# Head of a fused attention and MLP kernel: the first weight piece moved to ScalarE's queue, the first tiles reordered, two copies split, one constant's place in GpSimd's order changed

## The chip, the cores and the metric

The kernel runs on one core of a Trainium2 chip. A time is the device time of one execution in microseconds (us). The kernel before took 146.25 us, the median of three runs (146.13 to 146.31).

The core has five engines with a queue of instructions each: TensorE (PE: matmuls, and PEld for its weight loads), VectorE (DVE), ScalarE (ACT), GpSimd (POOL) and SyncE (SP, which here only issues DMAs). They meet through semaphores alone. Each engine takes its own instructions strictly in the order in which they were emitted, so an instruction that waits holds up everything behind it on its engine.

## The reference

One input x of 2048 tokens by 448 channels (bf16) is normalised, and two branches are computed from the result and added to x:

```
xn  = layernorm(x)
A   : q, k, v = xn @ wqkv (16 heads of 28); pq = q @ w_phi, pk = k @ w_phi (one 28x28 per head)
      phi = [softmax(p), softmax(-p)];  kv = phi_k^T v;  z = sum(phi_k)
      o = (phi_q kv) / (phi_q z + 1e-6);  A = o @ wo
B   : B = silu(xn @ w1) @ w2            (448 -> 1792 -> 448)
out = x + A + B
```

## The kernel before

Tokens are handled in 16 tiles of 128. The first tiles go a way of their own, the head; the rest of the work follows a list of blocks written out by hand (`PLAN`).

**Layer norm of a tile** (`ln_tile`, lines 699 to 744). VectorE computes the statistics (`bnst`, L702, and `bnag`, L703). For tiles 0 to 3 ScalarE takes the square root (`ve`, L706) and VectorE its reciprocal (`rstd`, L708); from tile 4 on GpSimd computes both `ve` (L711) and `rstd` (L713). VectorE then writes the normalised tile (`xn`, L717). Tiles 0 to 3 are turned over by TensorE, four transposes each (`tr`), which land in PSUM and are copied to `xnT` by ScalarE (`ev0a`, `ev0`, `ev1`, `ev2`) or, for tile 3, by VectorE (`ev3`). From tile 4 on, pairs of tiles are turned over by DMA transposes that SyncE issues (`xnT_dma5`, `xnT_dma7` and so on).

**The head on TensorE.** 38 matmuls of 128 columns on a tile of ones come first (`warm`, L586); nothing reads them. Then come the transposes, and, token tile by token tile, the first three blocks of `xn @ w1` (blocks 0, 1 and 2, two output tiles of 128 channels each). The order is one string (L1039): `00a` is block 0, token tile 0, contraction steps k = 0 and 1; `00b` is its last step, which takes k = 2 for one output tile and k = 3 for the other; `20` is block 2, tile 0, all steps. Blocks 0 and 1 read the first piece of w1 (columns 0 to 511), in two DMAs: `w1_0` (k = 0 and 1) and `w1_0r` (k = 2 and 3), 256 KB each. Block 2 reads the second piece, `w1_512` (k = 0 to 2, 384 KB) and `w1_512r` (k = 3, 128 KB).

**DMA issues.** SyncE issues, in this order, x0, x1 (112 KB each), x2 (tiles 2 and 3, 224 KB), w1_0, w1_0r, w1_512r, x4 (tiles 4 to 7, 448 KB), the rest of w1, the value weights, x8 and x12, and the transposes. ScalarE issues w1_512 behind its first activation table load and the small activation `warm_act`. GpSimd issues the four small loads of w_phi.

**The fold.** q and k are never formed: w_phi is folded into wqkv on the chip. GpSimd builds block-diagonal copies of w_phi (`bdphi`, L632, and `bd0`, L636), once the four loads of w_phi have landed. TensorE multiplies them with transposed pieces of wqkv (`fold_k`, words f0 and f1 in `PLAN`, L666), ScalarE copies out one reference column, and VectorE subtracts it (`fold_sub`, L695) into `Wqk`. Both f0 and f1 write PSUM banks 6 and 7, so f1 waits until f0's subtractions have read them.

**Order.** A small list scheduler (L228) puts the instructions in order by modelled times; its `chain` calls and the order of `PLAN` on TensorE are constraints on it. TensorE's order is fully written out. On VectorE, ScalarE and GpSimd it is written out for the first four tiles (L1025, L1026) and chosen by the scheduler's model behind them. GpSimd's order before has `bdphi` ahead of tile 4's `ve` and `bd0` ahead of its `rstd`. In `PLAN`, `aFn@b` and `bFn` are the two halves of block n of `xn @ w1`, seven blocks to each 512 tokens: F8 reads tiles 4 to 7, F25 reads tiles 12 to 15.

Of the kernel before, what the change touches and what calls it, by code (L numbers as in the profile page):

```python
# [358 lines left out]
SIGNAL = {("act", "pe"): 60.0, ("act", "dve"): 40.0, ("dve", "pe"): 100.0, ("dve", "sp"): 30.0, ("dve", "dve"): 34.0,  # L359
          ("pool", "pe"): 100.0}  # L360
PLAN = """r0 aF3@4 r2 r1 bF3 aF6@0 aF4@6 bF6 bF4 aF5@4 av2@2 av0@0 bv2 bF5 av4@6 bv0 bv4 aF10@2 aF9@0 bF10 f0@6 bF9 aF12@4 aF7@2
aF11@0 f1@6 bF11 bF7 bF12 aF25@0 ak2@6 bF25 bk2 av8@4 av12@2 bv8 ak0@0 bv12 bk0 av10@6 aF22@4 bv10 aF17@2 bF22 av14@6
aF14@0 bF17 bv14 aF18@4 bF14 aF27@6 ak4@2 bF27 bF18 bk4 av6@6 ak6@0 ak8@4 bv6 bk8 bk6 ak12@2 aF8@6 bk12 bF8 aY0@45
aF21@0 aY0 aF23@2 bF21 bF23 ak14@6 bY0 g0@1 bk14 bY0 aF13@0 aF19@2 bF13 aF20@4 bF19 aF24@6 bF20 bF24 ak10@0 g1@3 bk10 K0
K6 K4 aq4@2 K12 aq8@4 bq4 K8 K2 s4 aq0@0 bq8 aq6@2 K14 bq0 bq6 bY1@45 K10 M aY1 aq2@2 aF26@0 s6 bq2 bY1 bF26 aG3@23 aY1
aU2@67 s8 aF15@0 bU2 s0 bF15 aF16@4 bG3 bF16 aU4@01 aq12@6 bU4 bq12 aU3@45 bG3 bU3 s2 aG3 aq10@0 aq14@6 bq10 s10 aW2@45
# [5 lines left out]
def bass_parallel_sum__linear_kernel_hedgehog__dense_activation_silu__prompt_kernel(  # L372
# [36 lines left out]
    with es:  # L409
# [143 lines left out]
        def load(dst, src, name, eng="sp", lat=1700.0):  # L553
            n = 2
            for _, cnt in list(dst.ap):
                n *= cnt
            P.dma(lambda e: e.dma_start(out=dst, in_=src), n / 280.0, writes=[dst], name=name, eng=eng, lat=lat)  # L557
# [24 lines left out]
        memset(Wp0[:], 0.0, 28, "wp_zero")  # L582

        P.cur_prio = 9
        for i in range(38):
            o = P.op("pe", 107.0, lambda e: e.matmul(banks[3][:, 0:128], ones_bf[:], ones_bf[:], start=True, stop=True),  # L586
                 reads=[ones_bf[:]], writes=[banks[3][:, 0:128]], name="warm", mode=128)
            o.words = 2
# [10 lines left out]
        def load_w1(c0, c1, eng="sp"):  # L599
            load_rows4(w1_sb[:, :, c0:c1], B_w1, c0, c1, f"w1_{c0}", eng)  # L600
# [1 line left out]
        load_x(0, 1)  # L602
        load_x(1, 2)
        load_x(2, 4)
        load(w1_sb[:, 0:2, 0:512], B_w1[0:256, 0:512].rearrange("(k p) f -> p k f", p=128), "w1_0")
        load(w1_sb[:, 2:4, 0:512], bass.AP(B_w1.tensor, B_w1.offset + 256 * FF, [[FF, 128], [64 * FF, 2], [1, 512]]), "w1_0r")
        load_w1(512, 1024, "act")
        load_x(4, 8)
        load_w1(1024, FF)
        load_rows4(wv_sb, A_wqkv, 2 * D, 3 * D, "wv")  # L610
# [88 lines left out]
        def ln_tile(t):  # L699
            xs = x_sb[:, t, :]  # L700
            sl = t % NXN
            P.op("dve", 590, lambda e: e.bn_stats(st6[:, t, :], xs), reads=[xs], writes=[st6[:, t, :]], name=f"bnst{t}", okeys_w=["ln"])  # L702
            P.op("dve", 170, lambda e: e.bn_aggr(mv[:, t, :], st6[:, t, :]), reads=[st6[:, t, :]], writes=[mv[:, t, :]], name=f"bnag{t}",  # L703
                 okeys_w=["ln"])
            if t < 4:
                P.op("act", 220, lambda e: e.activation(ve[:, t:t + 1], mv[:, t, 1:2], ACTF.Sqrt, bias=epst[:]),  # L706
                     reads=[mv[:, t, 1:2], epst[:]], writes=[ve[:, t:t + 1]], name=f"ve{t}", table="sqrt", okeys_r=["sq"])
                P.op("dve", 120, lambda e: e.reciprocal(rstd[:, t:t + 1], ve[:, t:t + 1]),  # L708
                     reads=[ve[:, t:t + 1]], writes=[rstd[:, t:t + 1]], name=f"rstd{t}")
            else:  # L710
                P.op("pool", 200, lambda e: e.tensor_scalar(ve[:, t:t + 1], mv[:, t, 1:2], EPS_LN, None, ALU.add),  # L711
                     reads=[mv[:, t, 1:2]], writes=[ve[:, t:t + 1]], name=f"ve{t}")
                P.op("pool", 570, lambda e: e.tensor_tensor(rstd[:, t:t + 1], ve[:, t:t + 1], neghalf[:], ALU.pow),  # L713
                     reads=[ve[:, t:t + 1], neghalf[:]], writes=[rstd[:, t:t + 1]], name=f"rstd{t}")

            def norm(dst, c0, c1, dur, tag=""):
                P.op("dve", dur, lambda e: e.tensor_scalar(dst, x_sb[:, t, c0:c1], mv[:, t, 0:1], rstd[:, t:t + 1], ALU.subtract, ALU.mult),  # L717
                     reads=[xs, mv[:, t, 0:1], rstd[:, t:t + 1]], writes=[dst], name=f"xn{t}{tag}")

            dstx = xnT[:, t, :, :]  # L720
            if t >= XN_DMA0:
                norm(xn_sb[:, sl, 0:KF], 0, KF, 370)
                norm(xn_sb[:, sl, KF:512], D - 128, D, 250)
                if t % 2:
                    dma_t(xnT[:, t - 1:t + 1, :, :].rearrange("p i k c -> p (i k) c"),
                          xn_sb[:, sl - 1:sl + 1, :].rearrange("p i c -> p (i c)"), 950.0, f"xnT_dma{t}", 1330.0, lat=850.0)
                return

            def turn_over(k0, k1, b, tag):
                tps = bank16[b][:, 128 * k0:128 * k1].rearrange("p (k c) -> p k c", k=k1 - k0)  # L730
                transposes([(tps[:, kt - k0, :], xn_sb[:, sl, KS[kt]:KS[kt] + 128]) for kt in range(k0, k1)], f"tr{tag}")
                if t < 3:
                    act(dstx[:, k0:k1, :], tps, ACTF.Identity, 128 * (k1 - k0), f"ev{tag}")
                else:
                    copy(dstx[:, k0:k1, :], tps, 128 * (k1 - k0), f"ev{tag}")

            if t == 0:
                norm(xn_sb[:, sl, 0:256], 0, 256, 290, "a")
                norm(xn_sb[:, sl, 256:D], 256, D, 275)
                turn_over(0, 2, 4, "0a")  # L740
                turn_over(2, 4, 5, "0")
            else:
                norm(xn_sb[:, sl, 0:D], 0, D, 390)
                turn_over(0, 4, (7, 4, 5)[t - 1], str(t))

        LOW, HIGH = slice(0, 64), slice(64, 128)

# [274 lines left out]
            ln_tile(t)  # L1022
        fold()
        act(warm_act[:], ones_bf[:, 0:4], ACTF.Silu, 4, "silu_table", table="silu", okeys_w=["sq"])
        chain("bnst0 bnag0 bnst1 bnag1 rstd0 xn0a xn0 rstd1 xn1 bnst2 bnag2 bnst3 bnag3 rstd2 xn2 rstd3 xn3 ev3".split())  # L1025
        chain("warm_act w1_512 ve0 ve1 ev0a ev0 ev1 ve2 ve3 ev2 silu_table".split())  # L1026
        byname = {o.name: o for o in P.ops}
        byname["w1_512"].deps.add(byname["warm_act"].id)
        byname["w1_512"].odeps -= byname["w1_512"].deps
        fold_loads()  # L1030

        chunk = [(fp, c) for c in range(NCH) for fp in range(FP)]
# [3 lines left out]

        head = [F(0, 0), F(1, 2), F(2, AUX)]
        seq = []
        for word in "tr0a tr0 tr1 00a 10a 01a 11a 00b 10b 01b 11b tr2 20 21 tr3 02 12 22 03 13 23".split():  # L1039
            if word[0] == "t":  # L1040
                seq.append(word)
                continue
            f, t = int(word[0]), int(word[1])
            n0 = len(P.ops)
            head[f][0](t * 128, t * 128 + 128, {"": (0, 1, 2), "a": (0, 1), "b": (2,)}[word[2:]])
            for n, o in enumerate(P.ops[n0:]):
                o.name = f"F{word}_{n}"
                seq.append(o.name)
# [4 lines left out]
        block_mask(mask2[:], 2 * DH, 2, KP)  # L1053
        memset(vaug[:, :, :, DH], 1.0, 2150, "vaug1")
        memset(KVm[:], 0.0, 464, "kvm0")
        chain(["vaug1", "kvm0", "wphi", "wphi1", "wphi2", "wphi3"])
        def k_block(t, b0):
            return proj_block(t, b0, True)

# [12 lines left out]
        ones_column(NEK, NT)  # L1072
        for o in P.ops[-2:]:
            o.deps.add(late)

        prev = [max(o.id for o in P.ops if o.eng == "pe")]

# [177 lines left out]
```

## Time and profile before

| | |
|---|---|
| median of three runs | 146.25 us |
| the profiled execution: time, span | 146.72 us, 145.5 us |
| busy: PE, DVE, ACT, POOL | 97%, 62%, 55%, 52% |
| granted TensorE clock over the span | 1.000 |
| first matmul of `warm`, first transpose, first product with w1 | 1.06, 5.07, 6.10 us |
| last matmul's end, last addition on VectorE | 143.5, 143.9 us |

The span runs from the first to the last instruction of the profiled execution; its time is 1.22 us longer, and the profiled execution is 0.47 us above the median. Times in the lines of the profile count from the start of the span. In a line of the timeline the first number is the start, the second how long it or the run of like instructions took (their number is behind the x), and the brackets give the engine's idle time just before it and what ended that. A busy TensorE doesn't mean a useful one: the matmuls of `warm` count too.

### The profile page before, as it was taken

To read this page: it belongs to the slowest core of one execution; us is meant where nothing else is said; L and a number is where in the kernel's file an instruction comes from. 1 tells how busy PE (TensorE), PEld (TensorE's weight loads), DVE (VectorE), ACT (ScalarE), POOL (GpSimd) and SP (SyncE) were. 2 spreads that over 40 slices of the span, in tenths; PEclk is the share of its full clock that TensorE was granted. 3 is DMA by queue.
4 is the path that set the end of the run, shared out by engine and by line. 5 is a ranking of instruction groups with operands and counts; after the bars stand their busy time and mean duration, and the time that the engine had idled before them with its cause. 6 is when DMAs were issued, how large, how long until landed. Compare 5 with 4: busy or idle time off the path is not lost.

```text
span 145.5 us, 4553 instructions
## 1 busy us (share of the span) xinstructions
PE 141.3 (97%) x1968; PEld 83.0 (57%) x1968; DVE 89.5 (62%) x195; ACT 79.5 (55%) x96; POOL 75.2 (52%) x95
## 2 busy tenths in 40 slices
PE   7989999899999999999999999999999999999994
PEld 7785444345444544477787655555555556555773
DVE  1957899610770059948139999927796374635533
ACT  4567856379997899979896949246530000000000
POOL 8807477720097007799944999992398600000000
DMA  4999969654990000000000059959989999743522
GB/s 103 346 342 264 266 142 138 133 106 68 337 293 7 0 2 5 0 0 5 0 5 5 0 89 179 137 109 181 76 163 171 206 196 176 117 76 72 165 95 63
DMA packets 44500, 17.59 MB, mean 121 GB/s; under 512 B 36912, under 2 KB 44096, under 8 KB 44480
## 3 DMA queue, kind: packets, MB, share of 16 engines
q1 hardware_dynamic: 41648, 15.09, 53.0%
q10 hardware_dynamic: 2704, 2.19, 5.4%
q8 instruction: 15, 0.25, 0.7%
q0 software_dynamic: 128, 0.03, 0.1%
q14 instruction: 5, 0.04, 0.1%
HBM read 6.57 MB, written 1.84 MB: 58 GB/s over the span
## 4 chain that ended last, share of the span: by engine, by line
PE 68%; DVE 18%; POOL 5%; DMA 4%; issue 3%; ACT 1%; DVEq 0%; POOLq 0%; ACTq 0%
PE psum L520 68%; DVE Rec L837 7%; DMA Wp<-in_A_w_phi_dram 4%; DVE RA L717 4%; DVE st L702 3%; DVE Rec L838 2%; POOL rstd L713 1%; POOL Wp L557 1%; DVE mv L703 1%; POOL vaug L550 1%; DVE Wqk L695 1%; ACT Ek_sb L543 1%; POOL ve L711 1%; POOL BD L632 0%; DVE Y_sb L949 0%
## 5 line engine op out<-in xcount | busy, mean ns | idle before, releaser
L520 PE MATMUL psum<-xnT,phT 64*128 64x512 bf16 (+1 forms) x428 | 46.9, 350 | 0.6 <-DMA phT<-in_B_w_dram 0.4
L520 PE MATMUL psum<-w_sb,hT 64*128 64x448 bf16 (+4 forms) x455 | 46.5, 341 | 0.0
L837 DVE TENSOR_REDUCE Rec<-Ek_sb 128x32 f32<-128x896 bf16 (+1 forms) x20 | 24.4, 1251 | 18.7 <-ACT Ek_sb L543 18.6
L543 ACT ACTIVATE hT<-psum 128x1024 bf16<-128x1024 f32 x28 | 27.7, 1024 | 11.3 <-PE psum L520 11.2
L520 PEld LDWEIGHTS psum<-w_sb,hT 64*128 64x128 bf16 (+1 forms) x455 | 23.6, 94 | 17.2 <-issue 0.2
L520 PEld LDWEIGHTS psum<-xnT,phT 64*128 64x128 bf16 (+1 forms) x428 | 22.4, 95 | 19.0 <-DMA phT<-in_B_w_dram 0.6
L874 POOL TENSOR_TENSOR RA<-Ek_sb,Rec 128x896 bf16<-128x896 bf16 x16 | 27.1, 1723 | 5.7 <-DVE Rec L838 4.9
L520 PE MATMUL psum<-Wqk,xnT 64*128 64x432 bf16 x224 | 24.4, 342 | 0.0
L543 ACT ACTIVATE Ek_sb<-psum 128x864 bf16<-128x864 f32 x24 | 20.3, 917 | 6.3 <-PE psum L520 4.2
L847 POOL TENSOR_TENSOR Ek_sb<-Ek_sb,Rec 128x896 bf16<-128x896 bf16 x8 | 13.4, 1698 | 17.8 <-DVE Rec L838 17.8
L520 PEld LDWEIGHTS psum<-Wqk,xnT 64*128 64x128 bf16 x224 | 11.1, 94 | 8.2
L543 ACT ACT_TABLE_LOAD x11 | 14.1, 1283 | 1.0 <-PEq L1240 0.8
L847 POOL TENSOR_TENSOR phT<-phT,Rec 128x896 bf16<-128x896 bf16 x8 | 13.4, 1700 | 1.5 <-issue 0.9
L520 PE MATMUL psum<-wv,xnT 64*128 64x448 bf16 x112 | 12.2, 349 | 0.0
L1001 DVE TENSOR_TENSOR x_sb<-psum,x_sb 128x448 bf16<-128x448 f32 (+2 forms) x13 | 7.2, 583 | 7.5 <-PE psum L520 7.4
L702 DVE BATCH_NORM_STATS2 st<-x_sb 128x6 f32<-128x448 bf16 x16 | 9.7, 604 | 3.1 <-DMA x_sb<-in_A_x_dram 3.1
L520 PE MATMUL psum<-wo_sb,vaug 64*128 64x448 bf16 (+2 forms) x102 | 11.3, 338 | 0.0
L717 DVE TENSOR_SCALAR RA<-x_sb,mv,rstd 128x384 bf16<-128x384 bf16 (+4 forms) x29 | 9.0, 349 | 2.3 <-POOL rstd L713 2.1
L980 DVE TENSOR_TENSOR vaug<-psum,rden 128x448 bf16<-128x448 f32 x16 | 9.2, 619 | 0.0
L837 DVE TENSOR_REDUCE Rec<-phT 128x64 f32<-128x1792 bf16 x4 | 8.0, 1990 | 1.8 <-ACT phT L543 1.8
L838 DVE RECIPROCAL Rec<-Rec 128x32 f32<-128x32 f32 (+1 forms) x24 | 8.8, 396 | 0.2
L520 PEld LDWEIGHTS psum<-wv,xnT 64*128 64x128 bf16 x112 | 5.4, 94 | 5.6 <-ACT vaug L543 0.5
(60 smaller groups left out, 108.9 us busy)
## 6 DMA issues: line engine op xcount, KB each, us to landing
out_dram<-x_sb ACTq DMA_DIRECT2D x15, 112.0 KB, 2.4
w_sb<-in_B_w_dram SPq DMA_DIRECT2D x1, 1568.0 KB, 7.9
x_sb<-in_A_x_dram SPq DMA_DIRECT2D x3, 448.0 KB, 6.5
wo_sb<-in_A_wo_dram SPq DMA_DIRECT2D x2, 336.0 KB, 7.5
phT<-in_B_w_dram SPq DMA_DIRECT2D x1, 576.0 KB, 7.8
phT<-in_B_w_dram SPq DMA_DIRECT2D x2, 256.0 KB, 4.4
phT<-in_B_w_dram ACTq DMA_DIRECT2D x1, 384.0 KB, 4.7
wv<-in_A_wqkv_dram SPq DMA_DIRECT2D x1, 336.0 KB, 7.8
```

What stands on the lines that cost most here:

```text
L520: r = e.matmul(dst, lhsT, rhs, start=st, stop=sp, skip_group_check=True)
L543: P.op("act", d_act(n), lambda e: e.activation(dst, src, func, scale=scale), reads=[src], writes=[dst], table=table, name=name, **keys)
L550: P.op(eng, d_pool(n, 0.5), lambda e: e.memset(dst, v), writes=[dst], name=name)
L557: P.dma(lambda e: e.dma_start(out=dst, in_=src), n / 280.0, writes=[dst], name=name, eng=eng, lat=lat)
L702: P.op("dve", 590, lambda e: e.bn_stats(st6[:, t, :], xs), reads=[xs], writes=[st6[:, t, :]], name=f"bnst{t}", okeys_w=["ln"])
L717: P.op("dve", dur, lambda e: e.tensor_scalar(dst, x_sb[:, t, c0:c1], mv[:, t, 0:1], rstd[:, t:t + 1], ALU.subtract, ALU.mult), reads=[xs, ...
L837: P.op("dve", 50 + 967 * n, lambda e: e.tensor_reduce(R2, E4, AXL.X, ALU.add), reads=[E4], writes=[R2], name="Ssum")
L838: P.op("dve", 135 + 210 * n, lambda e: e.reciprocal(R2, R2), reads=[R2], writes=[R2], name="Rrec")
L847: P.op("pool", 1700, lambda e: e.tensor_tensor(E3, E3, Rk[:, :, None].broadcast_to([128, 32, DH]), ALU.mult), reads=[E3, Rk], writes=[E3], ...
L874: P.op("pool", 1700, lambda e: e.tensor_tensor(dst, Eq, Rq.rearrange("p (c j) -> p c j", c=CC)[:, :, :, None].broadcast_to([128, CC, 4, DH ...
L980: P.op("dve", 620, lambda e: e.tensor_tensor(o3, U3[:, :, 0:DH], rden[:, uq, :, None].broadcast_to([128, H, DH]), ALU.mult), reads=[U3[:, ...
L1001: P.op("dve", d_dve(cs.stop - cs.start), lambda e: e.tensor_tensor(res[:, cs], ob, addend[:, cs], ALU.add), reads=[ob, addend[:, cs]], wri ...
```

## The change

- The number of `warm` matmuls goes from 38 to 36.
- `w1_0` is issued by ScalarE, as its first instruction and ahead of its table load, once GpSimd's `ident` is done. `w1_512`, which ScalarE issued behind `warm_act`, goes to SyncE, between w1_0r and w1_512r.
- The copies of tiles 1 and 2 out of PSUM are split into two (`ev1a` and `ev1`, `ev2a` and `ev2`): k = 0 and 1, then k = 2 and 3.
- The order of the head on TensorE becomes tile 0 whole, tile 1, tile 2; tile 2's first part stands ahead of tile 3's transposes. On VectorE tile 3's `bnag` goes behind tile 2's `rstd` and `xn`.
- On GpSimd, `bdphi` and `bd0` go behind tile 7's `rstd`, and tile 8's `ve` behind them.
- In `PLAN`, F8 and F25 change places.

```diff
-aF11@0 f1@6 bF11 bF7 bF12 aF25@0 ak2@6 bF25 bk2 av8@4 av12@2 bv8 ak0@0 bv12 bk0 av10@6 aF22@4 bv10 aF17@2 bF22 av14@6
-aF14@0 bF17 bv14 aF18@4 bF14 aF27@6 ak4@2 bF27 bF18 bk4 av6@6 ak6@0 ak8@4 bv6 bk8 bk6 ak12@2 aF8@6 bk12 bF8 aY0@45
+aF11@0 f1@6 bF11 bF7 bF12 aF8@0 ak2@6 bF8 bk2 av8@4 av12@2 bv8 ak0@0 bv12 bk0 av10@6 aF22@4 bv10 aF17@2 bF22 av14@6
+aF14@0 bF17 bv14 aF18@4 bF14 aF27@6 ak4@2 bF27 bF18 bk4 av6@6 ak6@0 ak8@4 bv6 bk8 bk6 ak12@2 aF25@6 bk12 bF25 aY0@45
...
-        for i in range(38):
+        for i in range(36):
...
-        load(w1_sb[:, 0:2, 0:512], B_w1[0:256, 0:512].rearrange("(k p) f -> p k f", p=128), "w1_0")
+        load(w1_sb[:, 0:2, 0:512], B_w1[0:256, 0:512].rearrange("(k p) f -> p k f", p=128), "w1_0", "act")
...
-        load_w1(512, 1024, "act")
+        load_w1(512, 1024)
...
-            def turn_over(k0, k1, b, tag):
+            def turn_over(k0, k1, b, tag, cut=None):
...
-                if t < 3:
-                    act(dstx[:, k0:k1, :], tps, ACTF.Identity, 128 * (k1 - k0), f"ev{tag}")
-                else:
-                    copy(dstx[:, k0:k1, :], tps, 128 * (k1 - k0), f"ev{tag}")
+                for a, b, part in ((k0, k1, ""),) if cut is None else ((k0, cut, "a"), (cut, k1, "")):
+                    if t < 3:
+                        act(dstx[:, a:b, :], tps[:, a - k0:b - k0, :], ACTF.Identity, 128 * (b - a), f"ev{tag}{part}")
+                    else:
+                        copy(dstx[:, a:b, :], tps[:, a - k0:b - k0, :], 128 * (b - a), f"ev{tag}{part}")
...
-                turn_over(0, 4, (7, 4, 5)[t - 1], str(t))
+                turn_over(0, 4, (7, 4, 5)[t - 1], str(t), 2 if t < 3 else None)
...
-        chain("bnst0 bnag0 bnst1 bnag1 rstd0 xn0a xn0 rstd1 xn1 bnst2 bnag2 bnst3 bnag3 rstd2 xn2 rstd3 xn3 ev3".split())
-        chain("warm_act w1_512 ve0 ve1 ev0a ev0 ev1 ve2 ve3 ev2 silu_table".split())
+        chain("bnst0 bnag0 bnst1 bnag1 rstd0 xn0a xn0 rstd1 xn1 bnst2 bnag2 bnst3 rstd2 xn2 bnag3 rstd3 xn3 ev3".split())
+        chain("w1_0 warm_act ve0 ve1 ev0a ev0 ev1a ve2 ev1 ve3 ev2a ev2 silu_table".split())
         byname = {o.name: o for o in P.ops}
-        byname["w1_512"].deps.add(byname["warm_act"].id)
-        byname["w1_512"].odeps -= byname["w1_512"].deps
+        byname["w1_0"].deps.add(byname["ident"].id)
+        byname["w1_0"].xfer, byname["w1_0"].lat = 0.0, 2800.0
...
-        for word in "tr0a tr0 tr1 00a 10a 01a 11a 00b 10b 01b 11b tr2 20 21 tr3 02 12 22 03 13 23".split():
+        for word in "tr0a tr0 tr1 00a 10a 00b 10b 01a 11a 01b 11b tr2 20 21 02a tr3 12a 22a 02b 12b 22b 03 13 23".split():
...
+        chain(["rstd7", "bdphi", "bd0", "ve8"])
```

The lines that set `xfer` and `lat` change only what the scheduler believes of that DMA. The `chain` of `vaug1` to `wphi3` moves in the file with the same names in it.

More of the change, by code (lines that the diff above doesn't have):

```diff
@@ L1055, in bass_parallel_sum__linear_kernel_hedgehog__dense_activation_silu__prompt_kernel @@
         memset(KVm[:], 0.0, 464, "kvm0")
-        chain(["vaug1", "kvm0", "wphi", "wphi1", "wphi2", "wphi3"])
         def k_block(t, b0):
@@ L1074, in bass_parallel_sum__linear_kernel_hedgehog__dense_activation_silu__prompt_kernel @@
             o.deps.add(late)
+        chain(["vaug1", "kvm0", "wphi", "wphi1", "wphi2", "wphi3"])
+        chain(["rstd7", "bdphi", "bd0", "ve8"])
         prev = [max(o.id for o in P.ops if o.eng == "pe")]
```

## The prediction, made before the result was known

> **What bounds the kernel now.** First the page: which engine is full.
>
> ```profile
> span 145.5 us, 4553 instructions
> PE 141.3 (97%) x1968; PEld 83.0 (57%) x1968; DVE 89.5 (62%) x195; ACT 79.5 (55%) x96; POOL 75.2 (52%) x95
> ```
>
> TensorE is busy almost throughout, so a gain must come from its idle time or from work taken off it. Taken off are two `warm` matmuls of 107 ns. Its waits name the idle time:
>
> ```profile
> PE psum L520 <- DMA phT<-in_B_w_dram: 0.4, 1, 0.4
> PE psum L520 <- DVE Wqk L695: 0.4, 1, 0.4
> ```
>
> Since matmul ends are modelled, I measure gaps from start to start, against a step of 0.056 us for 128 columns and 0.216 for 512. From 5.7 us to the end three gaps exceed 0.24 us by that measure: 0.25 at 6.79 and 0.56 at 7.82 in the head, and 0.54 at 27.88. The timeline shows them with their causes:
>
> ```profile
> 0.80 1.28 ACT L543 ACT_TABLE_LOAD   x1 [0.80 <-PEq L1240]
> ...
> 2.10 0.20 ACT L543 ACTIVATE warm_act<-ones_bf 128x4 f32<-128x4 bf16 x1
> 2.20 1.46 SPq L557 DMA_DIRECT2D phT<-in_B_w_dram  x3
> 2.33 0.43 ACTq L557 DMA_DIRECT2D phT<-in_B_w_dram  x1
> ...
> 3.83 0.29 ACT L706 ACTIVATE ve<-mv,epst 128x1 f32<-128x1 f32 x1 [1.53 <-DVE mv L703]
> ...
> 6.10 1.31 PE L520 MATMUL psum<-xnT,phT 128*128 128x128 bf16 x16
> ...
> 6.79 0.45 PEld L520 LDWEIGHTS psum<-xnT,phT 128*128 128x128 bf16 x8 [0.26 <-ACT xnT L543]
> ...
> 7.82 0.62 PE L520 MATMUL psum<-xnT,phT 128*128 128x128 bf16 x8 [0.40 <-DMA phT<-in_B_w_dram]
> ```
>
> At 6.10 the first product starts just behind w1_0, whose last part the trace lands at 5.97; at 6.79 TensorE waits for ScalarE's copy of tile 1; at 7.82 for w1_0r, landed at 7.77. The third gap comes from a chain that starts on GpSimd:
>
> ```profile
> 11.62 0.56 POOL L632 TENSOR_TENSOR BD<-Wp,mask_half 128x224 bf16<-128x224 bf16 x1 [4.80 <-DMA Wp<-in_A_w_phi_dram]
> ...
> 12.16 0.23 POOL L711 TENSOR_SCALAR ve<-mv 128x1 f32<-128x1 f32 x1
> ...
> 12.61 0.57 POOL L713 TENSOR_TENSOR rstd<-ve,neghalf 128x1 f32<-128x1 f32 x1
> ...
> 13.22 0.60 DVE L717 TENSOR_SCALAR RA<-x_sb,mv,rstd 128x384 bf16<-128x384 bf16 x2 [0.91 <-POOL rstd L713]
> ```
>
> ```profile
> 26.71 1.12 DVE L695 TENSOR_TENSOR Wqk<-psum,last_k 128x432 bf16<-128x432 f32 x2
> ```
>
> ```profile
> 27.88 0.20 PE L520 MATMUL psum<-BD,Y_sb 64*128 64x56 bf16 x1 [0.38 <-DVE Wqk L695]
> ```
>
> GpSimd stands at `bdphi` until the w_phi loads are in (the last that it needs lands at 11.45), so tile 4's `ve` waits behind it, VectorE idles 0.91 us, and twelve tiles of layer norm run nearly without a break into f0's subtractions, which end at 27.83. There f1 starts, 0.54 us after TensorE was ready. From 28 us on I find no gap above 0.24, and the loads that land later do so long before their use.
>
> **The change part by part.**
>
> *Two `warm` matmuls less.* They end at 4.88 instead of 5.07. The transposes behind them wait for `xn0a`, which ends at 4.89: worth 0.1 us at most there, and nothing at the path, since tile 1's transposes at 5.71 wait for `xn1`.
>
> *w1_0 on ScalarE.* `ident` ends at 1.38, so the issue runs from about 1.45 for the 0.43 us of ScalarE's present one, instead of starting at 2.20. The table load is pushed from 0.80 to 1.88 and `warm_act` ends near 3.39, while the first `ve` is due at 3.83: cover 0.44 us, gone if an issue there takes 0.87 (GpSimd's take 0.52 to 0.98). The row of the load charges 1.28 us and the activation follows 0.01 us later. [...]
>
> *SyncE.* It still issues six DMAs ahead of x4, so x4 stays at 3.70 and nothing behind it moves. w1_0r goes from 2.68 to 2.20, w1_512 from ScalarE's 2.33 to 2.68. Bytes of w1 ahead of the end of w1_0r fall by 384 KB, 1.1 us at 342 GB/s. The DMA engines were not at full rate early:
>
> ```profile
> 2.50:3.00 0.50, 0.50 (x8) 0.50 (x6) 0.11 (x1) 0.00 (x0) 0.50 (x3) 1.00 1.05 226
> 3.00:3.50 0.50, 0.50 (x8) 0.50 (x7) 0.50 (x1) 0.00 (x0) 0.50 (x5) 1.00 0.72 154
> 3.50:4.00 0.50, 0.50 (x7) 0.50 (x6) 0.47 (x3) 0.17 (x1) 0.50 (x3) 1.00 1.02 342
> ```
>
> (The last number is GB/s, the one before it the engines' share.) Filled to 342, these two stretches give 0.15 MB more, 0.45 us off everything behind; by their share alone only 0.14 us. I take 0.25, ends 0 and 0.45. w1_0r then lands at 7.77 - 1.1 - 0.25 = 6.4 (6.2 to 6.7), w1_512r, last of the same bytes, at 8.16 - 0.25 = 7.9. In return w1_0 runs beside x1 and x2. Of x1, landing at 3.31 and used at 3.65, eight packets per DMA engine could each wait for one of w1_0's, 0.05 us apiece: 0.4 at worst, 0.34 covered. x2 lands at 4.41 and is used at 5.57; 256 KB ahead cost 0.75, covered.
>
> *The head's new order.* Replayed from rows: tile 1's transposes end at 5.94 by the step; 00a and 10a run 5.94 to 6.39 (w1_0 is in, 0.16 gained). 00b and 10b need w1_0r, 6.4 with a little signal: to 6.65. 01a, 11a need `ev1a`, 0.38 us from 6.14, done 6.52: to 7.10. 01b, 11b need `ev1`, behind `ve2`: 6.50 to 6.79, then 6.70 to 7.07: to 7.33. tr2 needs `xn2`, 0.15 earlier than its 7.61 since `bnag3` went behind it: 7.52 to 7.75. 20 and 21 to 8.42, their last step needing w1_512r (7.9 against 8.03). 02a to 8.65; tr3 needs `xn3`, about 8.57, so 0.45 later than now but hidden; 12a to 22b to 9.65, with `ev2` done at 8.6; tile 3's 18 products wait for `ev3` (about 9.5) and end at 10.65. Now they end at 11.40. The head gains 0.75; with w1_0r and w1_512r as late as 6.7 and 8.2 it is 0.5. The two extra copies cost ScalarE 0.16 us each, hidden: its next work is r0's output, and the silu table is in 0.6 us earlier than now.
>
> *bdphi and bd0 behind tile 7's rstd.* Tile 4's statistics end at 11.07, `ve` and `rstd` take 0.23 and 0.57, so `xn4` could go at 12.1; VectorE is through `bnst6` at 12.22. It starts there instead of 13.22, 1.0 us earlier, and the rest of the chain, VectorE's own work, follows; the 0.60 us wait at 16.13 for tile 7's `rstd` stays. If x4 lands 0.25 earlier than 10.20, so does all this: 1.25 (1.0 to 1.45). x8 lands at 15.24, used at 16.65 now and 15.4 then: no limit. What is put off is `bdphi`: ready near 15.5, used by f0 at 23.6.
>
> *f1.* TensorE's own path brings it 0.54 + 0.75 = 1.29 earlier, VectorE's 1.25. The later decides: 1.25, ends 1.0 and 1.3. Neither part alone would give that: with the head's gain alone f1 would wait for VectorE as now, gain 0; with GpSimd's alone 0.54.
>
> *F8 for F25.* Now F25 starts at 30.69 and its last transposed tiles land at 30.15. Earlier by 1.25 it would come at 29.4 against 28.9, which moves with VectorE; F8's tiles are in by 20.5. The swap costs and gains nothing, a cover of 0.5 us made wider. Its new place, 53.5, is long past all landings.
>
> *Behind f1* TensorE follows its fixed order; ScalarE is caught up there (idle 1.68 us ahead of its 28.30) and VectorE's stretch from 78 to 93.5 starts from TensorE's own products. I take off 0.1 for what new choices of the scheduler may cost. Sum: 1.15. For the profiled execution that is a span of 144.35 and a time of 145.57; it lies 0.47 above the median, so for the median 146.25 - 1.15 = **145.1 us**.
>
> **The rivals.**
>
> *The weights still come late.* If the DMA engines serve ScalarE's and SyncE's pieces mixed and w1_0r or w1_512r come near their old times, the head keeps 0.2 and f1 moves 0.54 + 0.2: 145.5. For it speaks that w1_512, issued 0.13 us behind w1_0, took until 7.03; against, that its 384 KB no longer stand ahead. It includes a table load placed ahead of the DMA, which would issue w1_0 at 2.1.
>
> *Given back later.* f1 comes earlier, but another order on VectorE or ScalarE makes TensorE wait elsewhere, above all at 93.5, which waits for VectorE, busy 16.4 of the 16.5 us before. One step of a tile's norm or one reduction (1.0 to 1.25 us) in the wrong place eats 0.8 to all of the gain: 145.9, up to 146.25. Against it: all that work is started by TensorE.
>
> *Cold clock.* `warm` steps by 107 ns, the transposes from 5.07 by 56: the rate doubled just as the 38 ended, 4.0 us after the first. If 36 with the pause behind them put this off by another such stretch, the head's matmuls up to about 9 us would step by 107 again; replayed so, it ends near 12.0 instead of 11.40, and f1 comes at 27.34 + 0.6 = 27.98, 0.1 later than now: 146.35. The granted clock in the rows is 1.00 and shows neither state. [...]
>
> *Slower: one more pair of activation tables.* ScalarE loads a table of 1.28 us eleven times, as the scheduler groups silu and exp. F25's silu now falls among k's exps at 53.5. If the new order splits a group there, two loads put 2.57 us into a stretch (41 to 77) where ScalarE is busy 31.6 of 35.9 us; with some 0.7 of its idle time at hand TensorE would wait 1.9: 147.0. It decides from a wait of 1.15 on; F8 sat in the same place with the same silu, which speaks against it.
>
> **How the numbers follow.** Forecast 0.60; weights late 0.15; given back 0.10, half of it within 0.2% of 146.25; cold clock 0.04; tables 0.08; better than 1.3, should f0's subtractions go ahead of the last tile's norm, 0.03. A change below 0.2% (0.3 us) can't be told from none here. Faster: 0.60 + 0.15 + 0.05 + 0.03 = 0.83; same 0.05 + 0.04 = 0.09; slower 0.08. The forecast's own range is 144.9 to 145.3; that of 8 in 10 reaches over the late weights and the better half of given back: 144.7 to 146.0.
>
> **What would show it.** Right: w1_0 issued by ACTq near 1.45 with the table load behind it; 00b without a wait at 6.4; r0 near 10.75 instead of 11.49; `xn4` near 12 with no `bdphi` ahead of it; f1 near 26.6 with almost no wait; from there the same gaps. Wrong: a first `ve` after 3.9, a wait for DMA above 0.3 in the head, f1's wait for VectorE above 0.3, a twelfth table load, or a gap above 0.3 behind 30 us.

## The result, and the profile after

The changed kernel takes 145.84 us (median of 8 runs, 145.66 to 145.94), the kernel before, run beside it, 146.26 us (8 runs, 146.13 to 146.40). The ratio is 0.9968 with a 95% interval of 0.9957 to 0.9979. Between the medians that is 0.42 us, where 1.15 was forecast. The direction was right and the time lies in the range of 8 in 10, but little more than a third of the gain came. Of the executions listed below, three of e4_dma_back and one of e5_after_again (147.95 to 150.28), each more than 1.5% above the fastest of its kernel, were in a slower state and are left out of the medians.

The profiled execution of the changed kernel took 145.75 us, inside the spread of its eight runs. The one of before that the prediction was worked from took 146.72, above all eight runs of the kernel before. Between these two executions the span shrank by 1.0 us, close to the 1.15 of the sum; between the medians, by 0.42. Most of what follows is about that difference.

The first lines of the page after:

```profile
span 144.5 us, 4551 instructions
PE 141.3 (98%) x1966; PEld 83.4 (58%) x1966; DVE 89.7 (62%) x195; ACT 79.7 (55%) x98; POOL 75.1 (52%) x95
```

TensorE has two matmuls less and the same busy time. Of its waits one is left, the one ahead of the first `warm`; the waits for w1 and for f0's subtractions, 0.4 us each before, are gone:

```profile
PE psum L586 <- POOL epst L550: 1.1, 1, 1.1
```

The timeline of after, with the steps that the prediction named:

```profile
1.41 0.43 ACTq L557 DMA_DIRECT2D phT<-in_B_w_dram  x1
...
1.87 1.28 ACT L543 ACT_TABLE_LOAD   x1 [1.87 <-POOL Wp L550]
...
3.16 0.20 ACT L543 ACTIVATE warm_act<-ones_bf 128x4 f32<-128x4 bf16 x1
...
3.89 0.29 ACT L706 ACTIVATE ve<-mv,epst 128x1 f32<-128x1 f32 x1 [0.53 <-DVE mv L703]
...
6.10 1.61 PE L520 MATMUL psum<-xnT,phT 128*128 128x128 bf16 x24
...
7.68 0.40 PE L537 MATMUL psum<-ident,RA 128*128 128x128 bf16 x4
...
11.56 0.59 DVE L717 TENSOR_SCALAR RA<-x_sb,mv,rstd 128x384 bf16<-128x384 bf16 x2
...
15.64 0.63 DVE L702 BATCH_NORM_STATS2 st<-x_sb 128x6 f32<-128x448 bf16 x1 [0.42 <-DMA x_sb<-in_A_x_dram]
...
26.90 0.19 PE L520 MATMUL psum<-BD,Y_sb 64*128 64x56 bf16 x1
```

ScalarE issues w1_0 at 1.41, the table load follows, and the first square root (`ve`) still starts as soon as its input is there. The 24 products of tiles 0 and 1 run without a wait from 6.10. `xn4` starts at 11.56 instead of 13.22, and f1 starts at 26.90 instead of 27.88, with no wait. VectorE has one new wait: at 15.64 it waits 0.42 us for x8.

### The profile page after: what moved, and what is told of

The parts are those of the page before. It is cut to its first block, busy times and chain, and to the rows that moved or that the text cites. A ratio compares the mean times of both kernels' runs of the same rounds, so it can differ in the third digit from the quotient of the medians.

```text
span 144.5 us, 4551 instructions
## 1 busy us (share of the span) xinstructions
PE 141.3 (98%) x1966; PEld 83.4 (58%) x1966; DVE 89.7 (62%) x195; ACT 79.7 (55%) x98; POOL 75.1 (52%) x95
## 4 chain that ended last, share of the span: by engine, by line
PE 83%; DVE 11%; issue 2%; DMA 2%; ACT 1%; ACTq 0%; DVEq 0%
PE psum L520 82%; DVE Rec L838 7%; DVE Rec L839 2%; DMA x_sb<-in_A_x_dram 2%; DVE st L702 1%; PE psum L537 1%; DVE RA L717 1%; ACT Ek_sb L543 1%; DVE Y_sb L950 0%; DVE kvsum L887 0%; DVE mv L703 0%; DVE x_sb L1002 0%; DVE rstd L708 0%; DVE KVm L889 0%; ACTq L1212 0%
```

## The experiments

Two of the marks in a trace turn out to say nearly everything: where TensorE starts **r0**, the first word of `PLAN`, and whether **f1** waits. From r0 on TensorE does the same work in every kernel here, and from r0 to the start of the last matmul the traces take 131.25 us (131.24 to 131.28 in eleven of fourteen). The three others are longer by a wait each: before, by 0.51 us (f1); e9, a kernel with late loads, by 0.35 (f1); after, by 0.14 (a value product at 19.64 for tiles 4 and 5, whose transposes land at 19.50). In the same way an execution's time is its r0 plus 134.70 us (134.67 to 134.73), plus such a wait. So every experiment can be read in one number. All times below are medians, in us; "before" is the kernel before in the same group.

| kernel | time | ratio to before, 95% interval | its trace: time of that execution, r0, wait at f1 (from start to start) |
|---|---|---|---|
| the kernel before, first profile | | | 146.72, 11.49, 0.54 |
| the change, first profile | 145.84 | 0.9968 (0.9957 to 0.9979) | 145.75, 10.91, 0 |
| e1_before_again | 146.09 | 0.9996 (0.9975 to 1.0018) | 145.96, 11.24, 0 |
| e2_pool_only | 146.21 | 1.0004 (0.9985 to 1.0023) | 146.15, 11.42, 0 |
| e3_no_pool | 146.31 | 0.9998 (0.9970 to 1.0027) | 146.06, 11.38, 0 |
| e4_dma_back | 146.61 | 1.0028 (1.0007 to 1.0049) | 146.79, 12.12, 0 |
| e5_after_again | 145.84 | 0.9976 (0.9958 to 0.9994) | 145.40, 10.73, 0 |
| e6_sp_all | 146.55 | 1.0015 (0.9990 to 1.0041) | 146.57, 11.86, 0 |
| e7_act_late | 146.18 | 0.9998 (0.9977 to 1.0019) | 146.42, 11.73, 0 |
| e8_no_swap | 146.26 | 1.0001 (0.9972 to 1.0031) | 145.67, 11.00, 0 |
| e9_wphi_late | 146.79 | 1.0027 (1.0006 to 1.0049) | 146.72, 11.66, 0.36 |
| e10_pool_wphi_late | 146.36 | 0.9986 (0.9969 to 1.0003) | 146.37, 11.64, 0 |
| e11_act_mid | 145.62 | 0.9941 (0.9918 to 0.9964) | 145.62, 10.95, 0 |
| e12_after_3 | 146.14 | 0.9980 (0.9948 to 1.0012) | 146.99, 12.31, 0 |

Three explanations were to be told apart. A: the prediction's, the head and f1's wait both give, and something ate the rest. B: f1's wait belonged to the one profiled execution and was not there to be won. C: w1_0 on ScalarE's queue brought nothing, and the new order alone does the work.

### Was the wait at f1 there to be won?

**The kernel before, again.** No edit.

> The kernel before, unchanged, for a second trace of it. Theory A (the trace shown before is typical, its 0.47 us above the median lies outside the kernel's own path): again a wait of about 0.5 us at f1 (0.75 from start to start), f1 near 27.9, the same span of 145.5. Theory B (the trace shown before was an execution whose wait at f1 was longer than usual, by the 0.47 us that it lies above the median): span about 145.0, f1 near 27.4 with a wait under 0.15, because the chain from the w_phi loads over GpSimd and VectorE, or the x4 load, came about 0.5 earlier. Ratio 1.000 by both.

Its TensorE waits, as the page lists them, in the trace of this second execution:

```profile
PE psum L586 <- POOL epst L550: 1.1, 1, 1.1
PE psum L520 <- ACT xnT L543: 0.2, 1, 0.2
```

And the chain around f1 in its timeline, the same instructions that the prediction showed:

```profile
10.76 0.56 POOL L632 TENSOR_TENSOR BD<-Wp,mask_half 128x224 bf16<-128x224 bf16 x1 [3.92 <-DMA Wp<-in_A_w_phi_dram]
...
12.35 0.60 DVE L717 TENSOR_SCALAR RA<-x_sb,mv,rstd 128x384 bf16<-128x384 bf16 x2 [0.59 <-POOL rstd L713]
...
25.83 1.11 DVE L695 TENSOR_TENSOR Wqk<-psum,last_k 128x432 bf16<-128x432 f32 x2
...
27.09 0.19 PE L520 MATMUL psum<-BD,Y_sb 64*128 64x56 bf16 x1
```

The same program, and f1 doesn't wait: the w_phi load that `bdphi` needs landed at 10.58 instead of 11.45, `xn4` started at 12.35 instead of 13.22, and f0's subtractions ended at 26.95, 0.14 us before TensorE came to f1. The wait is real in the first trace and absent in the second.

**GpSimd's order alone.** The kernel before with the one line of the change that puts `bdphi` and `bd0` behind tile 7's `rstd`:

```diff
+        chain(["rstd7", "bdphi", "bd0", "ve8"])
```

> The kernel before with one part of the change alone: bdphi and bd0 behind tile 7's rstd on GpSimd, tile 8's ve behind them; no other engine's order differs. Theory A: VectorE's chain comes 1.0 earlier, f1 no longer waits, 0.54 faster: 145.7. Theory B: the typical execution had next to no wait at f1 to win back, 0 to 0.15 faster: 146.1 to 146.25.

```profile
11.93 0.59 DVE L717 TENSOR_SCALAR RA<-x_sb,mv,rstd 128x384 bf16<-128x384 bf16 x2
...
27.27 0.19 PE L520 MATMUL psum<-BD,Y_sb 64*128 64x56 bf16 x1
```

The line does just what the prediction said it does: `xn4` at 11.93, f1 without a wait. And the time is that of before: 146.21 against 146.17, a difference of -0.22 to +0.34 by the interval. Behind r0 its trace takes the same 131.24 us as the others, so the line costs nothing there that could hide a gain. A wait at f1 in the median of before can therefore be 0.22 us at most, and the best estimate is none. A's 145.7 fell; B stands, for the kernel before.

**The change without that line.**

> The changed kernel with bdphi and bd0 at their old place on GpSimd; no other engine's order differs. Theory A: f1 waits for VectorE as in the first trace, all of the head's gain is lost there: 146.25, same as before. Theory B: likewise f1 waits for VectorE, but from a typical start; with x4 landing 0.7 earlier in the changed kernel the chain may come 0.2 to 0.4 earlier, so 145.9 to 146.2. A rival to both (GpSimd's place doesn't matter, the loads do): 145.84, as the full change.

146.31, 0.9998 of before. Its trace has no wait at f1, but it shows another late landing, x1 at 4.29 where before had 3.31:

```profile
4.32 0.63 DVE L702 BATCH_NORM_STATS2 st<-x_sb 128x6 f32<-128x448 bf16 x1 [0.54 <-DMA x_sb<-in_A_x_dram]
```

```profile
5.74 1.05 PE L537 MATMUL psum<-ident,RA 128*128 128x128 bf16 x8 [0.65 <-DVE RA L717]
```

VectorE, ahead of tile 1's statistics, waits 0.54 us, and since its order has them ahead of tile 0's norm, TensorE's first transposes come 0.65 late. Read literally, the ratio says that GpSimd's line is worth 0.4 us inside the changed kernel and nothing in the old one. With r0 some 0.4 us earlier and VectorE's chain no earlier, f1 would indeed come to wait in some executions. The trace shows no such wait, but only because its r0 is late (11.38): f0's subtractions end at 27.15, 0.08 us before f1 starts, and with the r0 of after (10.91) and this same end f1 would wait 0.4. So the line may be what lets the head's gain through, as the prediction said of the two parts. The intervals of this kernel and of the change overlap, and that stays open.

**The cause of the wait, made on purpose.** The kernel before with 1.2 us more of GpSimd's work ahead of its four w_phi loads (a memset that is done twice), without and with the change's line:

```diff
-        chain(["vaug1", "kvm0", "wphi", "wphi1", "wphi2", "wphi3"])
+        P.op("pool", 45.0, lambda e: e.memset(vaug[:, :, :, DH], 1.0), writes=[vaug[:, :, :, DH]], name="vaug2")
+        chain(["vaug1", "kvm0", "vaug2", "wphi", "wphi1", "wphi2", "wphi3"])
```

> The kernel before with one more memset of 1.2 us on GpSimd ahead of the four w_phi loads (it writes the same ones again); every engine's order is else the same. If the wait at f1 in the first trace came from w_phi's landing (11.45 there, 10.58 in the second trace, where f1 waited for nothing with 0.09 us to spare), the loads now land near 11.6 to 12, tile 4's norm near 13.4 to 13.8, f1 waits 0.8 to 1.1, and the kernel is 0.8 to 1.1 slower than before: 147.1. If w_phi's landing is not what f1 waited for, same as before.

```profile
11.55 0.56 POOL L632 TENSOR_TENSOR BD<-Wp,mask_half 128x224 bf16<-128x224 bf16 x1 [4.00 <-DMA Wp<-in_A_w_phi_dram]
...
13.15 0.60 DVE L717 TENSOR_SCALAR RA<-x_sb,mv,rstd 128x384 bf16<-128x384 bf16 x2 [0.98 <-POOL rstd L713]
...
27.88 0.20 PE L520 MATMUL psum<-BD,Y_sb 64*128 64x56 bf16 x1 [0.20 <-DVE Wqk L695]
```

The wait is back (0.36 us by starts), with the same `bdphi` in front of it, and the kernel takes 146.79 against 146.41. The cost is 0.4 us and not the 0.8 to 1.1 expected: the memset delayed the loads' landing (11.38) by 0.8 against the second trace of before, and r0 at 11.66 gave f1 more slack.

> The same late w_phi loads with bdphi and bd0 behind tile 7's rstd. The chain of layer norms no longer passes the loads, which are due only near 15: f1 waits for nothing, same as before, 146.2, some 0.9 faster than the run with the old order on GpSimd. If the place on GpSimd has no effect even then: as slow as that run.

```profile
12.07 0.59 DVE L717 TENSOR_SCALAR RA<-x_sb,mv,rstd 128x384 bf16<-128x384 bf16 x2
...
27.49 0.19 PE L520 MATMUL psum<-BD,Y_sb 64*128 64x56 bf16 x1
```

With the line, the same late load (11.54) costs nothing: 146.36 against e9's 146.79. This pair shows the mechanism: late w_phi loads hold up `bdphi`, `bdphi` holds up tile 4's norm, and that chain reaches f1. The line is an insurance against late loads. In the kernel before they were late in the profiled execution, and seldom enough that the median doesn't show it. Of its 100 executions in the three groups here, 17 took 146.72 us or more; how many of these waited at f1 is not known.

### What in the head gives?

**The load's move taken back, the new order kept.**

```diff
-        load(w1_sb[:, 0:2, 0:512], B_w1[0:256, 0:512].rearrange("(k p) f -> p k f", p=128), "w1_0", "act")
+        load(w1_sb[:, 0:2, 0:512], B_w1[0:256, 0:512].rearrange("(k p) f -> p k f", p=128), "w1_0")
...
-        load_w1(512, 1024)
+        load_w1(512, 1024, "act")
...
-        chain("w1_0 warm_act ve0 ve1 ev0a ev0 ev1a ve2 ev1 ve3 ev2a ev2 silu_table".split())
+        chain("warm_act w1_512 ve0 ve1 ev0a ev0 ev1a ve2 ev1 ve3 ev2a ev2 silu_table".split())
```

> The changed kernel with the loads as before (w1_0 on SyncE ahead of w1_0r, w1_512 on ScalarE behind warm_act); the head's new order, the split copies and GpSimd's new order stay. By the old landings w1_0r comes at 7.77, and the new order needs it 0.2 us after w1_0: TensorE waits 1.4 us at 00b and the head ends near 11.8, 0.4 later than before; f1 near 27.7 by TensorE's own path. Theory A: 0.2 slower to 0.2 faster than before, 146.1 to 146.4. Theory B: 0.3 to 0.4 slower, 146.6. Rival (ScalarE's early w1_0 hurts, since it delayed x0, x1 and x2 by 0.12, 0.25 and 1.34 in the changed kernel's trace): faster than the full change, under 145.84.

```profile
8.01 1.05 PE L520 MATMUL psum<-xnT,phT 128*128 128x128 bf16 x16 [1.47 <-DMA phT<-in_B_w_dram]
```

The new order asks for w1_0r right behind tile 0's first products, and w1_0r lands at 7.88, much as before (7.77): TensorE waits 1.47 us, and the kernel loses 0.44 (146.61 against 146.17). The order needs the loads.

**All of w1 on SyncE's queue, in the order of use.** ScalarE issues none.

```diff
-        load(w1_sb[:, 0:2, 0:512], B_w1[0:256, 0:512].rearrange("(k p) f -> p k f", p=128), "w1_0", "act")
+        load(w1_sb[:, 0:2, 0:512], B_w1[0:256, 0:512].rearrange("(k p) f -> p k f", p=128), "w1_0")
...
-        chain("w1_0 warm_act ve0 ve1 ev0a ev0 ev1a ve2 ev1 ve3 ev2a ev2 silu_table".split())
+        chain("warm_act ve0 ve1 ev0a ev0 ev1a ve2 ev1 ve3 ev2a ev2 silu_table".split())
...
-        byname["w1_0"].deps.add(byname["ident"].id)
-        byname["w1_0"].xfer, byname["w1_0"].lat = 0.0, 2800.0
```

> The changed kernel with all of w1's first two pieces on SyncE in the order w1_0, w1_0r, w1_512, w1_512r; ScalarE sends none, x4 is issued 0.47 later. Theory C (the early w1_0 brought nothing: it landed at 5.94 against 5.97, since it shares the DMA engines with x0, x1 and x2, which came 0.12, 0.25 and 1.34 later; what counts is that w1_512 no longer stands ahead of w1_0r): x1 at 3.3, x2 at 4.4, w1_0 near 5.4, w1_0r near 6.4, tile 1's transposes 0.1 earlier and tile 2's 0.2 earlier than in the changed kernel; 0.1 to 0.2 faster than it, 145.6. If the early issue is what helps, w1_0 comes near 6 and w1_0r at 7, and it is 0.3 to 0.5 slower than the changed kernel.

146.55 against 145.84 for the change in the same group. w1_0 landed early enough (5.47), but w1_0r came at 7.25 and w1_512 at 8.60, where after's trace has 6.52 and 7.66. SyncE issues w1_0r 0.48 us later, having one DMA more to issue, which is some two thirds of the 0.73 and half of the 0.94. The rest is seen in the stretches from 5 to 6 us (the last number is GB/s, the one before it the DMA engines' share). With SyncE alone:

```profile
5.00:5.50 0.50, 0.50 (x5) 0.27 (x4) 0.45 (x3) 0.07 (x1) 0.50 (x2) 1.00 0.90 213
5.50:6.00 0.50, 0.44 (x6) 0.31 (x5) 0.50 (x2) 0.50 (x2) 0.50 (x2) 1.00 0.53 164
```

and in the changed kernel:

```profile
5.00:5.50 0.50, 0.43 (x5) 0.31 (x4) 0.46 (x4) 0.00 (x0) 0.50 (x2) 1.00 1.07 358
5.50:6.00 0.50, 0.43 (x6) 0.19 (x4) 0.48 (x2) 0.43 (x2) 0.50 (x2) 1.00 1.05 358
```

C fell: issuing w1_0 from ScalarE's queue, early and without taking SyncE's time, is worth 0.71 us between these medians (the two intervals just touch). The 0.71 lies between the 0.48 us by which w1_0r is issued later (2.68 instead of 2.20) and the 0.8 of w1_0 itself (2.20 instead of 1.41); whether the later issues are all of it was not shown. The landings are those of single traces: in e12, a later trace of the changed kernel, the same two loads came at 7.08 and 9.15. All three traces of the change move 323 GB/s or more in both stretches from 5 to 6 us. Why the stream of SyncE's queue alone breaks off there was not found.

**w1_0 on ScalarE, but behind the table load and `warm_act`**, issued at 2.33 instead of 1.41:

```diff
-        chain("w1_0 warm_act ve0 ve1 ev0a ev0 ev1a ve2 ev1 ve3 ev2a ev2 silu_table".split())
+        chain("warm_act w1_0 ve0 ve1 ev0a ev0 ev1a ve2 ev1 ve3 ev2a ev2 silu_table".split())
...
-        byname["w1_0"].deps.add(byname["ident"].id)
+        byname["w1_0"].deps.add(byname["warm_act"].id)
+        byname["w1_0"].odeps -= byname["w1_0"].deps
```

> The changed kernel with w1_0 issued by ScalarE behind warm_act (at 2.33, where w1_512 was) instead of ahead of the table load; the rest as changed. Theory C: x0 to x2 as before; w1_0 and w1_0r share the engines and land near 6.4 both, so the first product starts 0.4 later than in the changed kernel, but tile 1 and 2 are in 0.1 to 0.2 earlier: the head ends 0.0 to 0.3 later, 145.9 to 146.1. If the early issue is what helps: 0.5 later, no gain over before.

146.18, no faster than before (146.28). w1_0, issued 0.13 us behind w1_0r, landed at 7.12 and w1_0r at 6.42: the piece issued first was served first, across two queues, and TensorE's first product waited until 7.16. That points to w1_0 standing first, not to the other queue as such, though the intervals of this kernel and of e5 overlap.

**w1_0 on ScalarE, a little later than in the change**: behind GpSimd's `wp_zero` rather than `ident`, so issued at 1.82 instead of 1.41, and thereby just behind SyncE's x2 (1.73).

```diff
-        byname["w1_0"].deps.add(byname["ident"].id)
+        byname["w1_0"].deps.add(byname["wp_zero"].id)
```

> The changed kernel with w1_0 issued 0.45 us later by ScalarE, behind x2's issue at 1.73 instead of ahead of it (it waits for a later memset of GpSimd), the table load still behind it. If the DMA engines serve the pieces in the order of issue, x1 and x2 land as before (3.3 and 4.4 instead of up to 4.3 and 5.6 to 6.1), tile 2's norm comes 0.2 earlier and executions with a late x1 go; w1_0 and w1_0r land near 5.7 and 6.6. The table load ends near 3.55, warm_act near 3.75, just ahead of the first square root. r0 near 10.6 to 10.9: 0 to 0.2 faster than the changed kernel. If the early first packet of w1_0 is what fills the engines, w1_0r comes near 7 and r0 near 11.2: 0.3 slower than it, same as before.

```profile
1.82 0.42 ACTq L557 DMA_DIRECT2D phT<-in_B_w_dram  x1
...
2.27 1.28 ACT L543 ACT_TABLE_LOAD   x1 [2.27 <-POOL maskh L573]
...
3.57 0.20 ACT L543 ACTIVATE warm_act<-ones_bf 128x4 f32<-128x4 bf16 x1
...
3.77 0.29 ACT L706 ACTIVATE ve<-mv,epst 128x1 f32<-128x1 f32 x1
...
6.00 1.51 PE L520 MATMUL psum<-xnT,phT 128*128 128x128 bf16 x24
```

145.62, the fastest kernel of the study: 0.9941 of before, and 0.5 us below the change in the same group (146.14), though the two intervals overlap a little (up to 0.9964, and from 0.9948). x2 landed at 5.13 instead of 5.75, w1_0 at 5.56. The first `ve` now follows `warm_act` directly at 3.77: its cover is gone to the last 0.01 us, and it still starts no later than before. But r0 comes at 10.95 in this trace, no earlier than in after or e5 (10.91 and 10.73), and its chain that ended last starts at w1_512r, which landed at 8.17:

```profile
3.19 4.98 DMA phT<-in_B_w_dram
...
8.22 0.79 PE psum L520 x11
```

Nor is its best execution better than the change's (145.43 against 145.40). The difference lies at the other end: the longest of its seven executions took 145.99, where e12 goes on to 147.70. What keeps it from longer ones, the trace doesn't show.

### The rest

**The change again**, twice.

> The changed kernel, unchanged, for a second trace and a time beside the variants of it. Theory B (against a typical execution of before, f1 has no wait to win back; only the head's gain counts, about 0.33 at the block r0, of which 0.13 goes at the first value block, which waits for the transposed tiles 4 and 5): 0.2 to 0.4 faster than before, r0 near 10.9, f1 near 26.9. If the early w1_0 makes x1 late in some executions, as in the trace without GpSimd's new order (x1 at 4.29 instead of 3.31, tile 0's transposes at 5.74), this trace may show it too, and then r0 comes near 11.4 and nothing is gained.

> The changed kernel once more, beside the run with the later w1_0. From the traces so far all that lies behind r0 takes 131.25 us with no extra wait, so the time follows r0: near 10.7 to 11.0 here, last matmul at 142.0 to 142.3, median 145.8 to 145.9, 0.2 to 0.4 faster than before.

145.84 and 146.14, 0.9976 and 0.9980 of before: the gain repeats at 0.3 to 0.4 us, in the second group not clear of none (up to 1.0012). Of the kernel's 32 timed executions the two profiled ones are the fastest and the third slowest. The first, 145.40, has the head as forecast: r0 at 10.73, with w1_0 in at 5.11. The second, 146.99, has r0 at 12.31, and TensorE waits for w1 twice, above all at block 2, as w1_512 landed at 9.15 instead of 7.66:

```profile
6.54 1.72 PE L520 MATMUL psum<-xnT,phT 128*128 128x128 bf16 x24 [0.22 <-DMA phT<-in_B_w_dram]
...
9.20 1.00 PE L520 MATMUL psum<-xnT,phT 128*128 128x128 bf16 x13 [0.59 <-DMA phT<-in_B_w_dram]
```

Same program, 1.6 us between them, all of it ahead of r0 and all of it in when DMAs landed.

**F8 and F25 back in their old places.**

> The changed kernel with F8 and F25 at their old places in PLAN. In the changed kernel's trace the block starts at 29.73 and tiles 12 to 15 are in at 29.07, so F25 there would wait for nothing in most executions: same as the changed kernel within 0.1. If the last transposes come 0.7 later in many executions, it is slower by part of that.

Inconclusive. The median is 146.26, but the times lie in two groups, five from 145.67 to 146.01 and five from 146.25 to 146.42 (two more near 147.7). The trace, of 145.67, has F25 start at 29.68 without a wait, its tiles having landed at 29.29, and 131.25 us behind r0 like the others. Nothing in it shows the swap to matter. In the other thirteen traces, too, these tiles are in before that block starts, by 0.2 to 1.4 us. The median says that the swap might matter, in executions that no trace shows.

## Why the prediction was right, and where it failed

**The step that failed first is f1's term, together with the move from the profiled execution to the median.** The prediction said "it lies 0.47 above the median, so for the median 146.25 - 1.15". Of the 1.15, some 0.4 to 0.5 was the wait at f1. But that wait, which made the stretch behind r0 0.51 us longer, is what made that execution 0.47 slower than the median: with r0 at 11.49 and no wait, 11.49 + 134.70 gives 146.19, the median itself. So the wait was subtracted from a time that didn't contain it. e1 shows an execution without it, e2 that removing it alone changes nothing in the median. Against its own execution the sum was nearly right: a span of 144.35 was forecast, 144.5 came. That match is partly luck, since the two later traces of the change have spans of 144.2 and 145.7.

**The second is the size of the head's gain, forecast as 0.75.** r0 was to come at 10.75; the traces of the change have 10.91, 10.73 and 12.31, those of before 11.49 and 11.24. In the first two the replay is right to within 0.2 us. But the medians correspond to r0 near 145.84 - 134.70 = 11.14 for the change and 146.26 - 134.70 = 11.56 for before, if neither median holds a wait at f1, so the typical gain of the head is 0.42. Together: the f1 term and the move to the median account for 0.35 of the miss of 0.74 us (10.75 + 134.70 = 145.45, not 145.1), the head for 0.39.

**Why the head gave less** is settled only in part. The first question is what limits it, and the chain that ended last tells, by line. In e1, an execution of before without the wait at f1, it starts from the weights:

```profile
PE psum L520 82%; DVE Rec L837 7%; DMA phT<-in_B_w_dram 3%; DVE Rec L838 2%; SPq L557 1%; ACT Ek_sb L543 1%; DVE Y_sb L949 0%; DVE kvsum L886 0%; PE psum L537 0%; DVE x_sb L1001 0%; DVE KVm L888 0%; ACTq L1209 0%; DVEq L1209 0%
```

After, it starts from x and its norm:

```profile
PE psum L520 82%; DVE Rec L838 7%; DVE Rec L839 2%; DMA x_sb<-in_A_x_dram 2%; DVE st L702 1%; PE psum L537 1%; DVE RA L717 1%; ACT Ek_sb L543 1%; DVE Y_sb L950 0%; DVE kvsum L887 0%; DVE mv L703 0%; DVE x_sb L1002 0%; DVE rstd L708 0%; DVE KVm L889 0%; ACTq L1212 0%
```

In order of time the load in it is x0 alone. From there it runs over VectorE's norm of tiles 0 and 1 to tile 1's transposes, and then along TensorE:

```profile
0.80 2.18 DMA x_sb<-in_A_x_dram
...
5.36 0.41 DVE RA L717
...
5.81 0.42 PE psum L537 x4
6.23 1.48 PE psum L520 x24
```

e5's chain is the same, with the transposes at 5.63. In these two executions the weights are no longer the limit, and r0 came at 10.91 and 10.73, as forecast. In other executions they still are: e12's r0 hangs on w1_512 (9.15), and that of e11, the variant with the later w1_0, on w1_512r. So what the typical execution lost against the forecast was probably lost by loads that landed later than in after and e5; which loads, and how often, the traces don't say, and the cause of these 0.39 us stays open.

One price of the move is clear, and it was mis-sized. With w1_0 issued at 1.41 (after, e3, e5, e8 and e12) x1 landed at 3.31 to 4.29, without that (before and seven more traces, with w1_0 issued at 2.2 or later) at 3.31 to 3.39. The prediction gave x1 "0.4 at worst"; it was 1.0 in e3, where 0.65 of it reached TensorE. For x2 it gave 0.75, covered: x2 landed at 5.57 to 6.29 in those five and at 4.41 to 4.94 in the eight others, so 1.2 to 1.9 later than in the trace of before (4.41). The cover was 1.16. In after and e5 that just sufficed, as x2 was in at 5.75 and 5.57 and VectorE came to it at 5.77 and 5.59; in e12 VectorE waited 0.66 us for it, but there w1_512 held TensorE longer. Whether x2 is part of what was lost is not shown: e11, which takes a part of that delay back (5.13), has the best median, but not the earlier r0 that would prove it.

The early DMA stream didn't fill up to 342 GB/s as assumed either; the same three stretches as in the prediction, in after:

```profile
2.50:3.00 0.50, 0.50 (x8) 0.50 (x6) 0.00 (x0) 0.50 (x1) 0.50 (x3) 1.00 0.85 192
3.00:3.50 0.50, 0.50 (x8) 0.50 (x7) 0.49 (x1) 0.35 (x2) 0.50 (x5) 1.00 0.77 112
3.50:4.00 0.50, 0.50 (x7) 0.50 (x6) 0.47 (x3) 0.11 (x1) 0.50 (x3) 1.00 0.74 193
```

so w1_0, issued 0.80 us earlier, landed at 5.94 against 5.97. What the new order of the loads did bring in after is w1_0r at 6.52 instead of 7.77 (forecast 6.4), and the last of w1 for block 2, w1_512r, at 8.04 instead of 8.16 (forecast 7.9).

Point by point, the other steps:

- *The table load and the first `ve`.* Right. The load takes 1.87 to 3.15, the activation starts at 3.16 and the first `ve` at 3.89. In the first traces of before and after each of the eleven loads (1.28 us) has its activation 0.01 us behind it. In e11, with no cover left, the load ends at 3.55, the activation starts at 3.57 and `ve` at 3.77.
- *GpSimd's order and `xn4`.* Right in after: 11.56 and 1.66 earlier than in the first trace of before, more than the 1.25 forecast, as x4 was in at 9.49 instead of 10.20. That is no gift of the change, as the forecast's 0.25 had it: e1, the kernel before, has x4 in at 9.52.
- *"x8 lands at 15.24 [...] no limit".* Wrong in after: x8 landed at 15.62, VectorE waited 0.42 for it, and tile 8's statistics came 1.0 earlier where tile 7's norm came 1.67 earlier. It cost nothing, since f0's subtractions ended at 26.82, ahead of f1 at 26.90.
- *F8 for F25, "nothing".* No trace contradicts it, e8's median does not support it; open.
- *Behind f1, 0.1 for the scheduler.* The same 131.25 us as before, but for 0.14 at one value product in one execution. *Given back later* did not happen, nor did *one more pair of activation tables*: ScalarE's count of instructions rose from 96 to 98, by the two copies alone.
- *Cold clock.* Steps of 0.107 us reached into the head in some executions, and cost next to nothing in the traces of the change. In after the transposes from 5.16 on step by 0.06, 0.11 and 0.11 us, and 0.056 holds only from 5.9 on. In e6 the first eight products take 1.01 us, where eight took 0.62 in the line of before at 7.82, since they step by 0.107 until 6.84:

```profile
6.09 1.01 PE L520 MATMUL psum<-xnT,phT 128*128 128x128 bf16 x8
```

There TensorE then waited for w1_0r (7.25) all the same; in after and e12 the slow steps lay ahead of waits too, but for 0.03 us. The kernel before has them as well (until 5.41 in e1, 6.05 in e2), so nothing shows that the two `warm` matmuls are the cause.
- *The weights still come late*, the rival of 145.5: not in after's trace, where no product waits for w1; but e12's is just that, at 146.99, so its price was too low. It was one of the three traces of the change; how often it comes is not known.
- *Two slips in the working.* 27.34 + 0.6 is 27.94, not 27.98, which makes that rival 146.31 instead of 146.35. And of the gaps above 0.24 us a fourth, 0.34, ends at 5.71, where tile 1's transposes wait for its norm. The prediction named that wait, but not as a limit; it is the one that bounds after and e5.

## What to carry to other kernels

Before a wait is priced from one profiled execution, compare that execution's time with the spread of the timed runs: where it lies above them all, as here, what makes it slow may be the very wait that looks winnable, and then it may not be subtracted from the median. Where everything behind one point runs without gaps, find that point and price only what moves it; here the whole study is the start of r0. When a load is moved ahead in one queue, ask which loads of the other queue it overtakes: the fastest version here (e11, 145.62) issued the first weights at 1.82, just behind the last load of x that the head needs (1.73).

## What the runs showed of the hardware

- **The load moved ahead on one queue delayed x2 on the other, but the order of issue alone didn't say which landed first.** x2, issued at 1.73 on SyncE's queue, landed at 4.41 to 4.94 in the eight traces with w1_0 issued at 2.2 or later, at 5.57 to 6.29 in the five with w1_0 at 1.41 on ScalarE's queue, and at 5.13 in e11, with w1_0 at 1.82. In e7 w1_0, issued 0.13 us behind w1_0r, landed 0.70 us after it. But in four of those five traces x2 landed ahead of w1_0, which had been issued 0.33 us earlier (5.75 against 5.94 in after).
- **The landings in the first microseconds varied from one execution to the next** by up to 1.7 us (w1_512 at 7.66, 7.49 and 9.15 in three executions of one program), and with them the time, by up to 1.6 us; behind r0 the traces agree to some 0.04 us but for the waits named.
- **The step of TensorE's matmuls halved, from 0.107 to 0.056 us for 128 columns, at a time that varied as well.** `warm` begins at 1.06 us with the longer one (1.07 in e7); the last step of that size ends at 3.71 in e9, 5.43 in after and 6.84 in e6. The granted clock in the rows reads 1.00 all the while.
- **All DMA nearly stopped between 14 and 15 us.** In both first traces a packet of 16 KB on queue q8, which the page lists as of the kind instruction (at 12.06 before, 12.54 after), is followed by 256-byte packets of the transposes that take up to 2.0 to 2.3 us, all ending together near 15.05 and 15.43, and x8 lands 0.19 us behind that, although in after the load ahead of it was in at 12.86. All fourteen traces have such a packet, between 12.0 and 13.5 us, and within 3.5 us behind its start a half microsecond of 37 GB/s or less. That this packet is the cause is a reading of their order, and was not tried. In that stretch before moved 37 GB/s, and after 18, in this row:

```profile
14.00:15.00 1.00, 1.00 (x12) 0.43 (x10) 0.54 (x2) 1.00 (x2) 1.00 (x3) 1.00 0.05 18
```
